# Decode attention with a gated MLP: one-hot products in place of small DMAs, and wq loaded in uneven strips

## The chip, the core and the metric

The kernel runs on one core of a Trainium2 chip. The metric is the device time of one execution in microseconds. A core has a matrix engine (PE, with weight loads listed as PEld), a vector engine (DVE), an activation engine (ACT), a general engine (POOL) and a queue engine (SP) which issues most of the DMAs. The DMAs run on 16 DMA engines. Matrix results land in PSUM; everything else is in SBUF, both with 128 partitions.

## The reference, cut to what matters

Two tokens (B = 2, one each) attend to a cache of 8 heads x 32,768 positions x 128, and the result is multiplied by a gate from a small MLP.

```python
x = A_x                                   # [2, 1, 512]
xn = _layernorm(x)
# attention: 32 query heads, 8 key/value heads, softmax over 32768 positions
q = (xn @ wq)                             # wq [512, 4096]
scores = einsum("bhqd,bhkd->bhqk", q, k) * Dh ** -0.5
o = einsum("bhqk,bhkd->bhqd", softmax(scores), v)
s = o.reshape(B, 1, Hq * Dh) @ wo         # wo [4096, 512]
# gate: an MLP on xn; with one position per token its token-mixing
# branch only sees the padding, so x1 = xn
h2 = _gelu(_layernorm(xn) @ w3) @ w4
g = _silu(xn + h2)
return x + s * g                          # [2, 1, 512]
```

## The kernel before

There are 16 groups, one for each pair of a token b and a key/value head k. The keys of a group are 32,768 x 128 bf16, 8 MB, and are laid out so that each partition holds 256 positions in a row of 65,536 bytes; the same goes for the values. The tile kbuf has three slots of 4 MB, vbuf two. One DMA of 128 rows loads the keys of a group (L398), one the values (L387); the last group is loaded in halves (L404, L392).

A loop on PE, DVE and ACT runs over the groups. DVE transposes blocks of the keys (L493), PE multiplies them with the query (L562), DVE finds the maxima (L476), ACT takes the exponential (L417), DVE turns the weights (L511), and PE multiplies them with the values (L584). PE's loop is one body that it branches back to; DVE's is a loop over pairs of groups; ACT, POOL and SP have their instructions written out for all groups.

The order of the loads is that of SP's queue. It first issues wq (L252) into the third slot of kbuf, w3 and w4 into vbuf (L253, L254) and the first keys (L255). Then, in turn, the values of a group, when PE has ended the products of the values before (L387, semaphore s_pv), and the keys of the next, when PE is half way through the scores (L398, semaphore s_half). Last come seven parts of wo (L411), the smaller ones at the end, and half of the store of the output (L523).

Before the loop comes a prologue. ACT's queue loads x (L258). DVE normalises it, PE turns it (L326) and multiplies it with wq, which waits for the semaphore of its load (L336); then come w3 (L357), a gelu, w4 (L372), and the gate g, two rows of 512 (L377). The output is computed in another layout: four partition quadrants, where partition 32n + b holds the columns 128n to 128n + 127 of token b. So x and g are needed there too. ACT's queue issues four DMAs of two rows for x into the tile x4_bf, which POOL has set to zero (L259, L270), and four of two rows for g into g4 (L267, L379). DVE casts x4_bf to f32 (L380).

The constants of the prologue are made by DVE from the identity matrix `ident` (L298 to L320).

After the loop PE computes the last head (L532) and multiplies the attention output with wo. The first KC = 2 of the eight row blocks of wo are multiplied in matmuls 512 wide into the PSUM tile qrb (L608); ACT copies that to SBUF as wsum (L519), and a product with `comb` brings it into the quadrants of `pro` (L623). The other blocks go straight into the quadrants, in matmuls 128 wide (L615). Each part waits for its own DMA. Then DVE multiplies with g4 and adds x4 (L520, L521), and SP and ACT store one token each (L523). The class LateQueue keeps PE's prologue instructions and places them ahead of the loop; a plain Queue records waits and counts.

Of the kernel before, what the change touches and what calls it, by code (L numbers as in the profile page):

```python
# [7 lines left out]
F32 = mybir.dt.float32  # L8
BF16 = mybir.dt.bfloat16
I32 = mybir.dt.int32  # L10
ACT = mybir.ActivationFunctionType
ALU = mybir.AluOpType
# [82 lines left out]
def kernel(  # L95
# [16 lines left out]
    B, Sq, D = A_x.shape  # L112
    _, Hkv, Sk, Dh = A_k_cache.shape
    HD = A_wq.shape[1]
# [4 lines left out]
    DK = D // 128  # L119
# [10 lines left out]
    NQ = 4  # L130
    QW = D // NQ
    QP = 32 * (NQ - 1) + B
# [6 lines left out]
    def sb(name, shape, dt):  # L139
        return pool.tile(shape, dt, name=name)  # L140
# [19 lines left out]
    xm = sb("xm", [128, NQ, rep], F32)  # L160
    z = sb("z", [128, NB, 2, ZC], BF16)
    x_bf = sb("x_bf", [B, D], BF16)
    x4_bf = sb("x4_bf", [128, QW], BF16)
    x4 = sb("x4", [128, QW], F32)
    g4 = sb("g4", [128, QW], F32)
    sg = sb("sg", [128, QW], F32)
    out4 = sb("out4", [128, QW], BF16)
    ident = sb("ident", [128, 128], BF16)
# [3 lines left out]
    cls = sb("cls", [128, NB, 2], F32)  # L172
    sel_o = sb("sel_o", [128, VT, rep], F32)
    quad = sb("quad", [128, 4], BF16)
    sel_h = sb("sel_h", [128, rep], F32)
    same_h = sb("same_h", [128, 128], F32)
    row_of = sb("row_of", [128, 32], F32)
# [20 lines left out]
    g = sb("g", [B, D], F32)  # L198
# [3 lines left out]
    sc = [bank(f"sc{i}") for i in range(NPART)]  # L202
# [4 lines left out]
    pro = bank("pro")  # L207
# [2 lines left out]
    groups = [(b, k) for b in range(B) for k in range(Hkv)]  # L210
    NG = len(groups)
    wo_parts = [(0, 4, 0, NQ), (4, 5, 0, NQ), (5, 6, 0, NQ), (6, 7, 0, NQ), (7, 8, 0, 2), (7, 8, 2, 3), (7, 8, 3, NQ)]
    KC = 2
    PAD = 24

    def sem(name):
        return tc.alloc_semaphore(name)

    def row_view(cache, b, k):
        return cache[b, k, :, :].rearrange("(p t) d -> p (t d)", p=128)  # L220

    sp = Queue(nc.sync, sem("s_sp"))
    ve = Queue(nc.vector, sem("s_ve"))
    ac = Queue(nc.scalar, sem("s_ac"))
    po = Queue(nc.gpsimd, sem("s_po"))
    pe = LateQueue(nc.tensor, sem("s_pe"))
    d_x, d_x4, d_wq, d_w3, d_w4, d_g, d_out = (
        sem(f"d_{n}") for n in ("x", "x4", "wq", "w3", "w4", "g", "out")
    )
    d_wo = [sem(f"d_wo{i}") for i in range(len(wo_parts))]  # L230
    t_T, t_z, t_mx, t_pt, t_ob, t_on = (sem(f"t_{n}") for n in ("T", "z", "mx", "pt", "ob", "on"))
    t_used, t_top, t_e, t_S, t_oT, t_xp = (sem(f"t_{n}") for n in ("used", "top", "e", "S", "oT", "xp"))
# [5 lines left out]
    kbuf_wq = kbuf[:, 2 * SLOT:3 * SLOT]  # L238
# [10 lines left out]

    with tc.tile_critical(sync_engine=mybir.EngineType.Pool, no_gpsimd_drain=True):  # L250

        sp.op(lambda e: e.dma_start(out=kbuf_wq[:, 0:DK * HD], in_=A_wq.rearrange("(p k) f -> p (k f)", k=DK)), inc=(d_wq, 16))  # L252
        sp.op(lambda e: e.dma_start(out=vbuf[:, 0:W4O], in_=B_w3.rearrange("(p k) f -> p (k f)", k=DK)), inc=(d_w3, 16))  # L253
        sp.op(lambda e: e.dma_start(out=vbuf[:, W4O:W4O + FK * D], in_=B_w4.rearrange("(p f) d -> p (f d)", f=FK)), inc=(d_w4, 16))  # L254
        sp.op(lambda e: e.dma_start(out=kbuf[:, 0:NPART * SLOT], in_=row_view(A_k_cache, *groups[0])), inc=(t_k[0], 16))  # L255
        nc.sync.sem_inc(t_k[1], 16)

        ac.op(lambda e: e.dma_start(out=x_bf[:, :], in_=A_x[:, 0, :]), inc=(d_x, 16))  # L258
        e_x4z = po.op(lambda e: e.memset(x4_bf[:, :], 0.0))  # L259
        e_xs0 = po.op(lambda e: e.memset(xs_bf[:, :], 0.0))  # L260
        e_id0 = po.op(lambda e: e.memset(ident[:, :], 0.0))
        e_id = po.op(lambda e: e.affine_select(
            out=ident[:, :], in_=ident[:, :], compare_op=ALU.not_equal, fill=1.0, base=0,
            pattern=[[-1, 128]], channel_multiplier=1), e_id0)
        e_ones = po.op(lambda e: e.memset(ones_f[:, :], 1.0))
        e_z0 = po.op(lambda e: e.memset(z[:, :, :, :], 0.0))
        e_g0 = po.op(lambda e: e.memset(g4[:, :], 0.0))  # L267
        po.op(lambda e: e.memset(ob[:, :], 0.0), inc=(t_ob, 1))
        for n in range(NQ):
            ac.op(lambda e, n=n: e.dma_start(out=x4_bf[32 * n:32 * n + B, :], in_=A_x[:, 0, n * QW:(n + 1) * QW]), e_x4z, inc=(d_x4, 16))  # L270


        ve.op(lambda e: e.memset(o[:, :], 0.0))
# [3 lines left out]
        e_s00 = ve.op(lambda e: e.memset(sc[1][:, :], 0.0))  # L277
        e = ve.op(lambda e: e.tensor_copy(out=xf[:, :], in_=x_bf[:, :]), (d_x, 16))
# [14 lines left out]
        e = e_xn = layernorm(xn, xf, "ln1", e)  # L293
        ve.op(lambda v: v.tensor_copy(out=xs_bf[0:B, :], in_=xn[:, :]), e_xn, e_xs0)
        e = layernorm(ln2, xn, "ln2", e_xn)
        e_xs = ve.op(lambda v: v.tensor_copy(out=xs_bf[32:32 + B, :], in_=ln2[:, :]), e)
        with nc.allow_low_precision(reason="one of the terms is one, the others are zero"):
            e = ve.op(lambda v: v.tensor_reduce(  # L298
                out=sel0[:, :], in_=ident[:, :].rearrange("p (n w e) -> p w n e", n=NB, e=2), axis=AX.XY, op=ALU.add), e_id)
# [6 lines left out]
            out=sel_o[:, :, :],  # L306
# [10 lines left out]
        ve.op(lambda v: v.tensor_scalar_mul(  # L317
            out=same_h[:, :].rearrange("p (r h) -> p r h", h=rep),
            in0=sel_h[:, :].unsqueeze(1).broadcast_to([128, 32, rep]), scalar1=-inv_sqrt_dh), e_selh)
        e_const = ve.op(lambda v: v.tensor_copy(  # L320
            out=sel_w[:, :, :], in_=row_of[:, :].unsqueeze(1).broadcast_to([128, 4, 32])), e_row)

# [9 lines left out]
        for i in range(NPART):  # L332
            for k in range(DK):
                for n in range(NQ):
                    last = k == DK - 1 and n == NQ - 1
                    e = pe.op(lambda t, i=i, k=k, n=n: t.matmul(  # L336
                        sc[i][32 * n:32 * n + B, :], lhsT=xT[:, k, :],
                        rhs=wq3[:, k, :].rearrange("p (h n y) -> p h n y", n=NQ, y=32)[:, i * HH:(i + 1) * HH, n, :],
                        start=(k == 0), stop=(k == DK - 1), tile_position=(0, 32 * n)),
                        e_xT, e_s00, (d_wq, 16), inc=last)  # L340
            e = ve.op(lambda v, i=i: v.transpose(out=qT[:, i * 512:(i + 1) * 512], in_=sc[i][:, :]), e)
        e_q = ve.op(lambda v: v.tensor_mul(
            out=q_sb[:, :, :, :].rearrange("p n e (b h) -> p (n e) b h", b=B),
# [31 lines left out]
        e_tf = ve.op(lambda v: v.tensor_add(out=t_f[:, :], in0=xn[:, :], in1=h2[0:B, :]), e_h2)  # L375
        e = ac.op(lambda v: v.activation(out=sig[:, :], in_=t_f[:, :], func=ACT.Sigmoid), e_tf)
        e_g = ve.op(lambda v: v.tensor_mul(out=g[:, :], in0=t_f[:, :], in1=sig[:, :]), e)  # L377
        for n in range(NQ):
            ac.op(lambda v, n=n: v.dma_start(out=g4[32 * n:32 * n + B, :], in_=g[:, n * QW:(n + 1) * QW]), e_g, e_g0, inc=(d_g, 16))  # L379
        e_x4 = ve.op(lambda v: v.tensor_copy(out=x4[:, :], in_=x4_bf[:, :]), (d_x4, 16 * NQ))  # L380
        ve.op(lambda v: v.memset(qrb[:, :], 0.0), e_qr)
        e_s0 = ve.op(lambda v: v.memset(pro[:, :], 0.0))

# [131 lines left out]
        e_oX[NG - 1] = head_out(last=True)  # L515


        e_ws, e_s = (pe.sem, pe.n + 1), (pe.sem, pe.n + 2)
        e_wsum = ac.op(lambda v: v.copy(out=wsum, in_=qrb[:, :]), e_ws)  # L519
        e = ve.op(lambda v: v.tensor_tensor(out=sg[0:QP, :], in0=pro[0:QP, 0:QW], in1=g4[0:QP, :], op=ALU.mult), (d_g, 16 * NQ), e_s)  # L520
        e = ve.op(lambda v: v.tensor_tensor(out=out4[0:QP, :], in0=sg[0:QP, :], in1=x4[0:QP, :], op=ALU.add), e, e_x4)  # L521
        for b, q in ((0, sp), (1, ac)):
            q.op(lambda v, b=b: v.dma_start(out=out[b, 0, :].rearrange("(n c) -> n c", c=QW), in_=out4[b:QP:32, :]), e, inc=(d_out, 16))  # L523
        sp.wait((d_out, 32))
# [2 lines left out]
        def head_oT(marks=None):  # L527
            take(nc.tensor, t_ob)
            for t in range(VT):
                if t == VT - 1 and marks:  # L530
                    marks.append(nc.tensor.mark_branch_hint_location())
                ins = nc.tensor.matmul(  # L532
                    oT[:, :], lhsT=ob[:, t * Dh:(t + 1) * Dh], rhs=sel_o[:, t, :],
                    start=(t == 0), stop=(t == VT - 1))
            ins.then_inc(t_oT, 1)
# [62 lines left out]
        with nc.body("pe_output", valid_engines=[PE]):  # L598

            marks = [nc.tensor.mark_branch_hint_location()]  # L600
            head_oT(marks)
            for i, (a, c, r0, r1) in enumerate(wo_parts):
                for k in range(a, c):
                    pe.wait(e_oX[(B - 1) * Hkv + k], (d_wo[i], 16))
                    for r in range(r0, r1):
                        gr = k * NQ + r
                        if k < KC:
                            pe.op(lambda t, k=k, r=r: t.matmul(  # L608
                                qrb[32 * r:32 * r + B, :], lhsT=oX[:, k, r, :], rhs=wo3[:, k, r * D:(r + 1) * D],
                                start=(k == 0), stop=(k == KC - 1), tile_position=(0, 32 * r)),  # L610
                                inc=(k == KC - 1 and r == NQ - 1))
                            continue
                        for n in range(NQ):
                            col = r * D + n * QW
                            pe.op(lambda t, k=k, r=r, n=n, col=col, gr=gr: t.matmul(  # L615
                                pro[32 * n:32 * n + B, 0:QW], lhsT=oX[:, k, r, :], rhs=wo3[:, k, col:col + QW],
                                start=(gr == KC * NQ), stop=(gr == Hkv * NQ - 1), tile_position=(0, 32 * n)),
                                inc=(gr == Hkv * NQ - 1 and n == NQ - 1))
                if i == 0:
                    take(nc.tensor, t_on)  # L620
                    head_xp()
                    for n in range(NQ):
                        pe.op(lambda t, n=n: t.matmul(  # L623
                            pro[32 * n:32 * n + B, 0:QW], lhsT=comb[:, :], rhs=wsum[:, n * QW:(n + 1) * QW],
                            start=False, stop=False, tile_position=(0, 32 * n)), e_wsum, inc=False)

            for _ in range(PAD):
                nc.tensor.wait_ge(d_wo[-1], 16)
            for n, mark in enumerate(marks):
                nc.tensor.br_ne(turn, 0, f"pe_output_{n}", "pe_groups").branch_hint(mark)  # L630
                nc.switch_bb(f"pe_output_{n}")
            nc.br("pe_done", engines=[PE])
# [31 lines left out]
```

## Time and profile before

| quantity | value |
|---|---|
| time, median of 3 runs | 657.79 us (657.18 to 658.07) |
| the profiled execution: its time, its span | 657.31 us, 655.5 us |
| granted PE clock, mean over the span | 0.81 |
| bytes read from HBM | 280.50 MB, 428 GB/s over the span |
| share of the 16 DMA engines' time on SP's queue (q1) | 99.0% |
| busy: PE, DVE, ACT, POOL | 409.6, 380.2, 39.5, 10.1 us |
| wq issued, first matmul that reads it | 0.89 us, 13.27 us |
| first values issued (L387) | 29.20 us |
| g sent to the quadrants (L379), four issues | 31.35 us, 2.50 us in all |
| wo issued: first part, seven issues | 616.81 us, over 22.97 us |
| multiply with g4, add of x4, store issued (start) | 651.55, 651.88, 652.19 us |

The span runs from the first to the last instruction of the profiled execution; what lies around it, 1.8 us, belongs to the time but is not in the profile. Times in the profile's lines are in microseconds, a mean in nanoseconds. In a line of the timeline the start comes first, then the duration, the engine, the line of the kernel, the operation, the tiles out<-in, the shape and the count; in brackets is the idle time of the engine before it and what ended it. "SPq" and "ACTq" are the queues that issue DMAs: their durations are the time of the issue, not of the transfer. In a table of stretches each row has the stretch, its length, the busy time of PE, PEld, DVE, ACT and POOL with counts, the granted clock, the busy share of the 16 DMA engines and the rate in GB/s.

The opening of the timeline, cut to the queues' issues and to the first matmul that reads wq:

```profile
0.89 0.39 SPq L252 DMA_DIRECT2D kbuf<-in_A_wq_dram  x1
0.90 0.55 ACTq L258 DMA_DIRECT2D x_bf<-in_A_x_dram  x1
1.34 0.41 SPq L253 DMA_DIRECT2D vbuf<-in_B_w_dram  x1
1.50 1.24 ACTq L270 DMA_DIRECT2D x_bf<-in_A_x_dram  x4
1.80 0.51 SPq L254 DMA_DIRECT2D vbuf<-in_B_w_dram  x1
2.35 0.52 SPq L255 DMA_DIRECT2D kbuf<-in_A_k_cache_dram  x1
13.27 3.58 PE L336 MATMUL sc<-kbuf,xT 128*2 128x512 bf16 x32 [4.07 <-DMA kbuf<-in_A_wq_dram]
29.20 0.33 SPq L387 DMA_DIRECT2D vbuf<-in_A_v_cache_dram  x1
31.35 2.50 ACTq L379 DMA_DIRECT2D g<-g  x4
```

### The profile page before, as it was taken

What the parts mean: (1) busy time and instruction counts of PE and PEld (TensorE: products, weight loads), DVE (VectorE), ACT (ScalarE), POOL (GpSimd) and SP (SyncE); (2) the same over time, 40 slices, a digit from 0 to 9 for tenths busy, and PEclk for the clock granted to TensorE, in tenths of its full rate; (3) what the DMA queues carried; (4) which work ended last, traced back from release to release, by engine and by line L of the source; (5) the groups of instructions that cost most, each with busy time, mean ns of one, the idle gap of its engine ahead of it and who ended that gap; (6) DMA issues with size and microseconds to landing.
All of it is one profiled execution on the core that took longest, in us unless ns stands there. A gap on an engine that the chain in (4) does not pass through costs nothing. (4 is left out here: it accounts for less than half of the span.)

```text
span 655.5 us, 6482 instructions
## 1 busy us (share of the span) xinstructions
PE 409.6 (62%) x2444; PEld 164.1 (25%) x2444; DVE 380.2 (58%) x534; ACT 39.5 (6%) x89; POOL 10.1 (2%) x43
## 2 busy tenths in 40 slices
PE   2528386564938656494765749566383856648765
PEld 0113132231313212131321313232131322213323
DVE  5348194673819457291855729285482937638770
ACT  1100101000010000001000000100001010000100
POOL 1000000000000000000000000000000000000000
PEclk9859677696987769697686969878696887979798
DMA  8999999999999999999999999999999999999996
GB/s 365 435 449 444 445 420 420 444 444 444 396 448 444 444 428 412 448 440 444 416 428 444 440 448 400 444 444 440 440 404 448 440 444 420 424 444 414 448 418 262
DMA packets 6779, 280.58 MB, mean 428 GB/s; under 512 B 746, under 2 KB 1012, under 8 KB 2036
## 3 DMA queue, kind: packets, MB, share of 16 engines
q1 hardware_dynamic: 6728, 280.50, 99.0%
q8 instruction: 2, 0.03, 0.0%
q14 instruction: 5, 0.04, 0.0%
q10 hardware_dynamic: 44, 0.01, 0.0%
HBM read 280.50 MB, written 0.00 MB: 428 GB/s over the span
## 5 line engine op out<-in xcount | busy, mean ns | idle before, releaser
L493 DVE STREAM_TRANSPOSE T<-kbuf 128x1024 int32<-128x1024 int32 x256 | 295.7, 1214 | 186.7 <-DVEq L473 186.4
L562 PE MATMUL sc<-T,z 128*128 128x512 bf16 x1024 | 280.2, 422 | 164.9 <-PEq L473 161.8
L562 PEld LDWEIGHTS sc<-T,z 128*128 128x128 bf16 x1024 | 98.8, 104 | 330.1 <-issue 251.7
L584 PE MATMUL o<-vbuf,pt 128*16 128x512 bf16 x1024 | 90.8, 533 | 35.0 <-PEq L473 35.0
L584 PEld LDWEIGHTS o<-vbuf,pt 128*16 128x16 bf16 x1024 | 34.3, 117 | 85.8 <-issue 78.4
L417 ACT ACTIVATE ep<-sc,shift 128x512 bf16<-128x512 f32 x32 | 21.7, 682 | 479.8 <-DVE shift L503 479.8
L511 DVE STREAM_TRANSPOSE pt<-ep 128x512 bf16<-128x512 bf16 x32 | 22.6, 708 | 15.3 <-DVEq L473 15.3
L476 DVE TENSOR_REDUCE mx<-sc 128x1 f32<-128x512 f32 x32 | 21.5, 672 | 15.7 <-DVEq L473 15.7
L574 PE MATMUL S<-mxr,same_h 128*128 128x64 f32 x32 | 6.5, 284 | 22.0 <-PEq L473 22.0
L532 PEld LDWEIGHTS oT<-sel_o,ob 128*128 128x128 f32 x136 | 17.7, 191 | 3.2 <-issue 0.5
L532 PE MATMUL oT<-sel_o,ob 128*128 128x4 f32 x136 | 16.2, 243 | 0.5 <-PEq L473 0.5
L420 ACT COPY ob<-o 128x512 f32<-128x512 f32 x16 | 9.4, 585 | 97.0 <-PE o L584 97.0
L574 PEld LDWEIGHTS S<-mxr,same_h 128*128 128x128 f32 x32 | 4.8, 188 | 29.8 <-issue 29.8
L438 POOL COPY oX<-oXs 128x4 bf16<-128x4 bf16 x15 | 2.8, 188 | 520.8 <-DVE oXs L470 520.8
L478 DVE TENSOR_SCALAR mxr<-row_of,mx 128x32 f32<-128x32 f32 x32 | 7.7, 241 | 4.8 <-DVEq L473 0.3
L503 DVE TENSOR_REDUCE shift<-S 128x1 f32<-128x64 f32 x16 | 3.6, 225 | 11.2 <-DVEq L473 11.2
L591 PEld LDWEIGHTS S<-sm,ones_f 128*128 128x128 f32 x32 | 4.8, 188 | 6.9 <-issue 6.9
L372 PE MATMUL sc<-vbuf,h_bf 128*2 128x512 bf16 x14 | 4.8, 521 | 2.4 <-DVE h_bf L369 2.4
L417 ACT ACTIVATION_READ_ACCUMULATOR ep<-sc,shift 128x1 f32 x32 | 6.3, 196 | 0.0
L427 POOL TENSOR_TENSOR z<-qr,quad 128x64 bf16<-128x64 bf16 x16 | 4.7, 292 | 102.2 <-DVE shift L503 86.4
L591 PE MATMUL S<-sm,ones_f 128*128 128x8 f32 x32 | 6.2, 266 | 0.0
L336 PE MATMUL sc<-kbuf,xT 128*2 128x512 bf16 x32 | 3.6, 627 | 4.1 <-DMA kbuf<-in_A_wq_dram 4.1
(88 smaller groups left out, 63.6 us busy)
## 6 DMA issues: line engine op xcount, KB each, us to landing
kbuf<-in_A_k_cache_dram SPq DMA_DIRECT2D x2, 4096.0 KB, 21.7
vbuf<-in_A_v_cache_dram SPq DMA_DIRECT2D x2, 4096.0 KB, 20.2
kbuf<-in_A_wq_dram SPq DMA_DIRECT2D x1, 4096.0 KB, 12.3
vbuf<-in_B_w_dram SPq DMA_DIRECT2D x2, 1792.0 KB, 18.0
kbuf<-in_A_wo_dram SPq DMA_DIRECT2D x1, 2048.0 KB, 29.3
kbuf<-in_A_wo_dram SPq DMA_DIRECT2D x3, 512.0 KB, 30.8
kbuf<-in_A_wo_dram SPq DMA_DIRECT2D x1, 256.0 KB, 31.7
kbuf<-in_A_wo_dram SPq DMA_DIRECT2D x2, 128.0 KB, 15.6
```

Of the source, the lines that this page charges most:

```text
L372: e_h2 = pe.op(lambda t, f=f: t.matmul(h2[0:B, :], lhsT=h_bf[:, f * B:(f + 1) * B], rhs=w4v[:, f, :], start=(f == 0), stop=(f == FK - 1)), ...
L417: ac.op(lambda v, i=i: v.activation(out=ep[i][:, :], in_=sc[i][:, :], func=ACT.Exp, scale=inv_sqrt_dh, bias=shift[:, :], accum_out=rs[:, i ...
L420: ac.op(lambda v: v.copy(out=ob[:, :], in_=o[:, :]), (s_pv, m + 1), inc=(t_ob, 1))
L476: nc.vector.tensor_reduce(out=mx[:, i:i + 1], in_=sc[i][:, :], axis=AX.X, op=ALU.max).then_inc(t_d, 1)
L478: ins = nc.vector.tensor_scalar_mul(out=mxr[:, i, :], in0=row_of[:, :], scalar1=mx[:, i:i + 1])
L493: nc.vector.transpose(out=Ts[n % T_BUFS][:, :].rearrange("p (b t k) -> p t b k", b=NB, t=RT), in_=kt[:, r * W:(r + 1) * W].rearrange("p (t ...
L511: nc.vector.transpose(out=pt[h][:, :, :].rearrange("p r (t h) -> p t r h", h=rep), in_=ep[order(par).index(h)][:, :].rearrange("p (t r h) ...
L532: ins = nc.tensor.matmul(oT[:, :], lhsT=ob[:, t * Dh:(t + 1) * Dh], rhs=sel_o[:, t, :], start=(t == 0), stop=(t == VT - 1))
L562: ins = nc.tensor.matmul(sc[i][:, :], lhsT=z[:, nb, w, zc:zc + 128], rhs=Tb[:, nb, :, w], start=(r == 0 and nb == 0 and w == 0), stop=(r = ...
L574: nc.tensor.matmul(S[:, NPART * rep:], lhsT=same_h[:, :], rhs=mxr[:, :, :].rearrange("p i r -> p (i r)"), start=True, stop=True).then_inc( ...
L584: ins = nc.tensor.matmul(o[32 * j:32 * j + VT * rep, :], lhsT=pt[h][:, r, a * VT * rep:(a + 1) * VT * rep], rhs=vt[:, u * VT:(u + 1) * VT, ...
L591: nc.tensor.matmul(S[:, 0:NPART * rep], lhsT=ones_f[:, :], rhs=sm[:, :, :].rearrange("p i h -> p (i h)"), start=True, stop=True).then_inc( ...
```

## The change

The eight small DMAs that bring x and g into the quadrants go, with the tile x4_bf, the two memsets on POOL and the cast on DVE. In their place PE multiplies, after the last head's products and ahead of wo, the rows of x with a piece of the identity (two ones, bf16), and the rows of g with the same in f32 (`one_f`, copied by DVE among the constants). Eight matmuls write x and g for the four quadrants into the PSUM bank sc[0]; ACT copies them into x4 and g4 ahead of wsum. The final multiply waits for these copies.

KC is 3 instead of 2: one more row block of wo goes through qrb and wsum.

The load of wq becomes 13 DMAs. One brings the first 8,192 of the 16,384 columns (16 KB of each partition's row) on 128 partitions. The rest comes in four strips of 2,048 columns (4 KB a row), each as a DMA of partitions 0 to 111 and two of the last 16 partitions, split 8 and 8, 12 and 4, 14 and 2, 10 and 6. The matmuls at L336 wait for all of them.

```diff
-    x4_bf = sb("x4_bf", [128, QW], BF16)
+    one_f = sb("one_f", [B, 32], F32)
...
-    KC = 2
+    KC = 3
+    CP = 2048
+    C0 = DK * HD - 4 * CP
+    wq_parts = [(0, 128, 0, C0)]
+    for i, r in enumerate((8, 12, 14, 10)):
+        wq_parts += [(a, b, C0 + i * CP, C0 + (i + 1) * CP) for a, b in ((0, 112), (112, 112 + r), (112 + r, 128))]
...
-        sp.op(lambda e: e.dma_start(out=kbuf_wq[:, 0:DK * HD], in_=A_wq.rearrange("(p k) f -> p (k f)", k=DK)), inc=(d_wq, 16))
+        for r0, r1, c0, c1 in wq_parts:
+            sp.op(lambda e, r0=r0, r1=r1, c0=c0, c1=c1: e.dma_start(
+                out=kbuf_wq[r0:r1, c0:c1], in_=A_wq.rearrange("(p k) f -> p (k f)", k=DK)[r0:r1, c0:c1]), inc=(d_wq, 16))
...
-        e_x4z = po.op(lambda e: e.memset(x4_bf[:, :], 0.0))
...
-        e_g0 = po.op(lambda e: e.memset(g4[:, :], 0.0))
...
-        for n in range(NQ):
-            ac.op(lambda e, n=n: e.dma_start(out=x4_bf[32 * n:32 * n + B, :], in_=A_x[:, 0, n * QW:(n + 1) * QW]), e_x4z, inc=(d_x4, 16))
...
+        ve.op(lambda v: v.tensor_copy(out=one_f[:, :], in_=ident[0:B, 0:32]))
...
-                        e_xT, e_s00, (d_wq, 16), inc=last)
+                        e_xT, e_s00, (d_wq, 16 * len(wq_parts)), inc=last)
...
-        for n in range(NQ):
-            ac.op(lambda v, n=n: v.dma_start(out=g4[32 * n:32 * n + B, :], in_=g[:, n * QW:(n + 1) * QW]), e_g, e_g0, inc=(d_g, 16))
-        e_x4 = ve.op(lambda v: v.tensor_copy(out=x4[:, :], in_=x4_bf[:, :]), (d_x4, 16 * NQ))
...
-        e_ws, e_s = (pe.sem, pe.n + 1), (pe.sem, pe.n + 2)
+        e_xg, e_ws, e_s = ((pe.sem, pe.n + i) for i in (1, 2, 3))
+        for t, dst in enumerate((x4, g4)):
+            e_x4 = ac.op(lambda v, t=t, dst=dst: v.copy(out=dst[:, :], in_=sc[0][:, t * QW:(t + 1) * QW]), e_xg)
...
-        e = ve.op(lambda v: v.tensor_tensor(out=sg[0:QP, :], in0=pro[0:QP, 0:QW], in1=g4[0:QP, :], op=ALU.mult), (d_g, 16 * NQ), e_s)
-        e = ve.op(lambda v: v.tensor_tensor(out=out4[0:QP, :], in0=sg[0:QP, :], in1=x4[0:QP, :], op=ALU.add), e, e_x4)
+        e = ve.op(lambda v: v.tensor_tensor(out=sg[0:QP, :], in0=pro[0:QP, 0:QW], in1=g4[0:QP, :], op=ALU.mult), e_x4, e_s)
+        e = ve.op(lambda v: v.tensor_tensor(out=out4[0:QP, :], in0=sg[0:QP, :], in1=x4[0:QP, :], op=ALU.add), e)
...
+            for t, (lhs, rhs) in enumerate(((ident[0:B, 0:32], x_bf), (one_f[:, :], g))):
+                for n in range(NQ):
+                    pe.op(lambda v, t=t, lhs=lhs, rhs=rhs, n=n: v.matmul(
+                        sc[0][32 * n:32 * (n + 1), t * QW:(t + 1) * QW], lhsT=lhs, rhs=rhs[:, n * QW:(n + 1) * QW],
+                        start=True, stop=True, tile_position=(0, 32 * n)), e_g, inc=t == 1 and n == NQ - 1)
```

More of the change, by code (lines that the diff above doesn't have):

```diff
@@ L226 @@
     pe = LateQueue(nc.tensor, sem("s_pe"))
-    d_x, d_x4, d_wq, d_w3, d_w4, d_g, d_out = (
-        sem(f"d_{n}") for n in ("x", "x4", "wq", "w3", "w4", "g", "out")
-    )
+    d_x, d_wq, d_w3, d_w4, d_out = (sem(f"d_{n}") for n in ("x", "wq", "w3", "w4", "out"))
     d_wo = [sem(f"d_wo{i}") for i in range(len(wo_parts))]
```

## The prediction

> **What bounds the kernel now.** First the page's engine shares and slices.
>
> ```profile
> span 655.5 us, 6482 instructions
> PE 409.6 (62%) x2444; PEld 164.1 (25%) x2444; DVE 380.2 (58%) x534; ACT 39.5 (6%) x89; POOL 10.1 (2%) x43
> DMA  8999999999999999999999999999999999999996
> DMA packets 6779, 280.58 MB, mean 428 GB/s; under 512 B 746, under 2 KB 1012, under 8 KB 2036
> ```
>
> No engine passes 62%, while the DMA engines are full in 38 of 40 slices. Next, the waits of the SP queue (time in total, times, longest) and the DMA issues with the median time to landing:
>
> ```profile
> SPq L387 <- PE o L584: 281.7, 14, 20.7
> SPq L398 <- PE sc L562: 229.9, 13, 19.0
> ...
> kbuf<-in_A_k_cache_dram SPq DMA_DIRECT2D x15, 27.2
> vbuf<-in_A_v_cache_dram SPq DMA_DIRECT2D x15, 26.4
> ```
>
> SP waits for PE before each load, but a load then needs 27 us to land while 8 MB takes 8 x 2.414 = 19.3 us per lane (below): some 8 us of earlier work is still queued at each issue, so the DMA engines never starve. The trace's packet records (queue, start, duration, bytes) show it finely. On one DMA engine the next packet starts 3 to 4 ns before the last one ends, so the records string into 16 lanes. In each, packets follow without a gap from 1.9 us to the end, and one costs about 5 ns + 0.0368 ns per byte: 65,536 B 2.414 us, 32,768 B 1.209, 4,096 B 0.155, a semaphore write 0.006. The end of the kernel is the end of the last lane. Busy time by stretch there (DMA share and GB/s are last):
>
> ```profile
> 649.00:649.25 0.25, 0.19 (x16) 0.00 (x0) 0.00 (x0) 0.00 (x0) 0.00 (x0) 1.00 1.06 377
> 649.25:649.50 0.25, 0.00 (x0) 0.00 (x0) 0.00 (x0) 0.00 (x0) 0.00 (x0) 1.00 0.86 307
> 649.50:649.75 0.25, 0.00 (x0) 0.00 (x0) 0.00 (x0) 0.00 (x0) 0.00 (x0) 1.00 0.69 225
> 649.75:650.00 0.25, 0.02 (x4) 0.05 (x6) 0.00 (x0) 0.00 (x0) 0.00 (x0) 1.00 0.23 82
> 650.00:650.25 0.25, 0.25 (x16) 0.19 (x16) 0.00 (x0) 0.00 (x0) 0.00 (x0) 1.00 0.20 70
> 650.50:651.00 0.50, 0.34 (x12) 0.19 (x12) 0.00 (x0) 0.00 (x0) 0.00 (x0) 1.00 0.09 35
> ```
>
> A share of 0.20 is three lanes of 16. Lane A ends at 650.91, B at 650.54, C at 650.31, the 13 others between 649.31 and 649.85; the mean is 649.72. The three are late because instruction fetches ran on them: 16,384 B at 71.9 us on A (0.96 us, and the packet after it took 2.886 instead of 2.418), 8,192 B at 35.8 us on B (0.31, then 2.955), 8,192 B at 265.3 us on C (0.31, then 2.662). C is also one of the two lanes (call them the pair) that carried every two-row DMA of L270 and L379. A's last packet frees the last matmuls, then VectorE and the store:
>
> ```profile
> 650.94 0.09 PEld L615 LDWEIGHTS pro<-kbuf,oX 128*2 128x2 bf16 x4 [0.21 <-DMA kbuf<-in_A_wo_dram]
> 651.55 0.29 DVE L520 TENSOR_TENSOR sg<-pro,g 98x128 f32<-98x128 f32 x1 [3.12 <-PE pro L615]
> 651.88 0.29 DVE L521 TENSOR_TENSOR out<-sg,x 98x128 bf16<-98x128 f32 x1
> 652.19 0.64 SPq L523 DMA_DIRECT2D out_dram<-out  x1
> ```
>
> From 650.91 to the span's end is 4.6 us. So the change is worth what it does to the last of 16 lane ends, and to this tail.
>
> **The strips of wq.** Half of wq goes in one DMA of 128 rows of 16 KB, eight rows per lane. The other half goes in four strips of 4 KB rows: each strip 112 rows (seven per lane), then r and 16-r rows with r = 8, 12, 14, 10, at most one row per lane. If a DMA of r rows takes the first r lanes of a fixed order, as the two-row DMAs always took the pair, the lanes get c = 8, 8, 7, 7, 6, 6, 5, 5, 3, 3, 2, 2, 1, 1, 0, 0 extra rows; an even split is 4. A lane's wq now costs 8 x 1.209 + 0.006 = 9.678 us. After: 8 x 0.607 (worked out from the 5 ns + bytes line) + (28 + c) x 0.1555 + (5 + c) x 0.006. The difference is -0.44 us at c = 0, +0.21 at the mean c = 4 (smaller packets), +0.69 at 7, +0.86 at 8. Every lane then carries its difference to the end, as it carries the fetches now.
>
> [...]
>
> **The DMAs of x and g that go.** Four of L270 and four of L379 put one row and one semaphore write each on both lanes of the pair: a 256 B row held the lane up by 14 ns, a 512 B row by 23, a write by 6. That is 4 x 20 + 4 x 29 = 0.20 us off the pair, nothing off A or B. The 2.5 us of issuing at L379 leave the ACT queue, which is next needed for the first group's Exp at 66.4 us (L417): no gain.
>
> **Sum of the lanes.** C, of the pair: 650.31 + 0.86 - 0.20 = 650.97. A is not of the pair: 650.91 plus -0.44 to +0.69, unknown where. B: 650.10 to 651.23. Others: at most 649.85 + 0.69 = 650.54. With A at c = 0 to 3 (four of seven values) C takes over and the end moves by +0.06; with c = 5, 6, 7 by +0.37, +0.53, +0.69. I take +0.06 and keep -0.44 (if C's fetch falls elsewhere) and +0.69 for the range.
>
> **Issue time on SP.** Twelve more DMAs at 0.39 to 0.64 us (L252 to L255 and L523) put the w3 issue at 0.89 + 13 x 0.45 = 6.7 us, or 9.2 at the dear end; 1.04 us from issue to first packet (0.89 to 1.93) makes 10.3. The lane with least work has wq until 1.9 + 0.7 (cold first packet) + 9.2 = 11.8. So w3, w4 and K0 queue in time; SP is next wanted at 29.20 (L387). Gone cover would cost up to 0.5 us. wq lands about 0.7 us later on the pair, so PE starts L336 at 14 instead of 13.27 and V0 is issued at 30 instead of 29.2; K0 occupies the lanes until 40.2.
>
> **Tail.** On PE, eight source matmuls go before L608: four bf16 like L615 (16 in 0.39: 0.10 us) and four f32 like L623 (eight in 0.40), 0.5 to 0.6 together. KC = 3 adds four 512-wide matmuls (eight took 0.60: +0.30) and removes sixteen 128-wide (-0.39).
>
> ```profile
> 646.24 0.60 PE L608 MATMUL qrb<-kbuf,oX 128*2 128x512 bf16 x8 [0.65 <-DMA kbuf<-in_A_wo_dram]
> 646.90 0.59 ACT L519 COPY T<-qrb 128x512 f32<-128x512 f32 x1 [2.47 <-PE qrb L608]
> 647.54 0.40 PE L623 MATMUL pro<-T,comb 128*2 128x128 f32 x8
> 648.79 0.39 PE L615 MATMUL pro<-kbuf,oX 128*2 128x128 bf16 x16 [0.63 <-DMA kbuf<-in_A_wo_dram]
> 649.98 0.39 PE L615 MATMUL pro<-kbuf,oX 128*2 128x128 bf16 x16 [0.80 <-DMA kbuf<-in_A_wo_dram]
> ```
>
> The one-hot products fit the 0.65 us that PE idles before L608. ACT copies two 128x128 tiles, each between 0.2 (a small ACTIVATE) and 0.59 (L519), while L608 runs; wsum then starts at about 647.2, L623 behind it at 647.9 instead of 647.5. PE idles 0.63, 0.80 and 0.25 us before later parts, so 1.7 us of slip is covered; without cover the tail would lengthen by at most 0.6 + 0.4 = 1.0. DVE (cast for cast) and POOL (two memsets fewer) are off the path.
>
> **Do the strips run at line rate?** Every load of before covers 128 partitions; seven rows per lane is shown nowhere. Lower bound: 0.155 us a row, as in the wo packets, +0. Upper bound from the slowest packets: the first sixteen of wq took 1.91 us on average instead of 1.213, a factor 1.57; on 32 x 0.155 = 4.98 us that is +2.8. Evidence for the lower end: the eight 512 B rows of g went, from the pair, into partitions that other lanes also write, and no K packet from 36.2 to 56.9 us took anything but 2.418. But 512 B might hide in a buffer. I take +0.
>
> [...]
>
> **Sum.** The profiled execution took 657.31 us (span 655.5, 1.8 around it): 657.31 + 0.06 = 657.37. The median of the three runs is 657.79, 0.48 above it: forecast 657.9, own range 657.3 to 658.5.
>
> **Rivals.**
> Lanes evened: C's fetch falls on another lane, or the extra rows do, and A and B are low in c. [...] The end falls by 0.44 and at best to the mean, 649.72 + 0.21, -1.0: 656.8 to 657.4.
> [...]
> Late tail: part 0 of wo no longer finds PE idle and the slip is not made good: up to +1.0, 658.9. Against: 1.7 us of idle PE behind.
> The change doesn't do what it says: the r rows spread evenly, c = 4 everywhere; then A ends +0.21 later, 658.0, inside the forecast's range.
>
> **How the numbers follow.** Forecast with its range (the even spread included) 0.47; slow strips 0.35; lanes evened 0.14; late tail 0.04. 0.2% is 1.3 us, about what a measurement of this kernel can tell from no change. Slower: slow strips and a part of the late tail, 0.38. Faster: evening cannot reach 656.5 by its own floor, but what the fetches do from run to run is unknown, 0.09. Same: 0.53. Range 656.9 to 661.0.
>
> **What would show it.** Lane ends: C near 650.97 as last or beside A; 4,096 B packets of wq at 159 ns (right) or 200 and more (slow strips); wq landing at 13.5; DMA share falling over 1.5 us at the end as before (right) or in under 0.8 (evened); idle PE before the later parts of wo. Packets of wq above 0.2 us would make the prediction wrong.

## The result, and the profile after

The changed kernel takes 660.90 us (median of 6 runs, 660.64 to 661.08) against 657.51 us of the kernel before in the same comparison: a ratio of 1.0051, with a 95% interval from 1.0038 to 1.0064. It is slower by 3.4 us. The profiled execution took 661.08 us, with a span of 658.8 against 655.5. One execution of a kernel further down (the same destination, another source) took 698.02 us, in a slow state, and is left out of its median.

The page after, engine shares and DMA:

```profile
span 658.8 us, 6485 instructions
PE 410.0 (62%) x2444; PEld 164.0 (25%) x2444; DVE 380.1 (58%) x534; ACT 39.9 (6%) x91; POOL 9.8 (1%) x41
DMA  9999999999999999999999999999999999999996
DMA packets 7386, 280.57 MB, mean 426 GB/s; under 512 B 850, under 2 KB 1108, under 8 KB 2644
```

Nearly the same bytes, and DMA engines as busy as before, in a longer span. Busy is not the same as moving. Busy time by stretch at the start shows it; the last two columns are the busy share of the DMA engines and GB/s. First, two stretches of the kernel before, while its one DMA of wq runs:

```profile
4.00:6.00 2.00, 0.00 (x0) 0.00 (x0) 1.52 (x6) 0.25 (x2) 0.00 (x0) 1.00 1.02 442
...
10.00:12.00 2.00, 0.00 (x0) 0.00 (x0) 0.73 (x6) 0.00 (x0) 0.00 (x0) 1.00 1.03 443
```

Then the changed kernel:

```profile
4.00:6.00 2.00, 0.00 (x0) 0.00 (x0) 1.52 (x6) 0.20 (x1) 0.00 (x0) 1.00 1.02 434
...
8.00:10.00 2.00, 0.29 (x4) 0.21 (x4) 1.93 (x11) 0.70 (x1) 0.00 (x0) 1.00 1.05 289
10.00:12.00 2.00, 0.00 (x0) 0.00 (x0) 0.64 (x6) 0.00 (x0) 0.00 (x0) 1.00 1.05 272
12.00:14.00 2.00, 0.00 (x0) 0.00 (x0) 0.00 (x0) 0.00 (x0) 0.00 (x0) 1.00 1.03 277
```

From 4 to 6 us the first half of wq comes in at 434 GB/s. While the strips run, all 16 lanes are busy, but at 272 to 289 GB/s: each packet takes longer. The trace's packet records (start, duration, bytes of each packet) give the size: the 512 packets of 4,096 B of the strips took 234 ns on the mean, where 159 is the undisturbed duration (893 of the 896 packets of that size in wo took it before). That is 75 ns x 32 packets = 2.40 us per lane. And the loss goes on into the next load: the packets of w3 and w4, all 535 ns before, cost 0.71 us more per lane, almost all of it in the first two of each lane. This outlasts the strips themselves: the last strip packet ended at 15.89 us, and a w3 packet that began at 15.93 still took 859 ns. The 16 lanes end at 652.85 us on the mean, 3.12 later than before, and the last one at 653.95, 3.04 later.

The timeline at the start and at the end (most lines are left out):

```profile
0.89 4.99 SPq L256 DMA_DIRECT2D kbuf<-in_A_wq_dram  x13
5.92 0.36 SPq L258 DMA_DIRECT2D vbuf<-in_B_w_dram  x1
16.93 3.58 PE L338 MATMUL sc<-kbuf,xT 128*2 128x512 bf16 x32 [7.89 <-DMA kbuf<-in_A_wq_dram]
...
648.57 0.23 PE L605 MATMUL sc<-x_bf,ident 2*32 2x128 bf16 x4
648.64 0.39 PE L605 MATMUL sc<-g,one_f 2*32 2x128 f32 x8
649.10 0.27 ACT L519 COPY x<-sc 128x128 f32<-128x128 f32 x1 [1.63 <-PE sc L605]
649.34 0.82 PE L614 MATMUL qrb<-kbuf,oX 128*2 128x512 bf16 x12 [0.31 <-DMA kbuf<-in_A_wo_dram]
650.84 0.40 PE L629 MATMUL pro<-T,comb 128*2 128x128 f32 x8 [0.35 <-ACT T L520]
653.06 0.39 PE L621 MATMUL pro<-kbuf,oX 128*2 128x128 bf16 x16 [0.84 <-DMA kbuf<-in_A_wo_dram]
654.60 0.23 PE L621 MATMUL pro<-kbuf,oX 128*2 128x128 bf16 x4 [0.36 <-DMA kbuf<-in_A_wo_dram]
```

The first matmul that reads wq starts at 16.93 us instead of 13.27. At the end the one-hot products lie ahead of the first part of wo, and PE still waits for a DMA before the later parts: the end is the end of the DMA stream, as before.

### The profile page after: what moved, and what is told of

Read it like the earlier page. It is cut to its first block, busy times and chain, and to the rows that moved or that the text cites. A ratio compares the mean times of both kernels' runs of the same rounds, so it can differ in the third digit from the quotient of the medians.

```text
span 658.8 us, 6485 instructions
## 1 busy us (share of the span) xinstructions
PE 410.0 (62%) x2444; PEld 164.0 (25%) x2444; DVE 380.1 (58%) x534; ACT 39.9 (6%) x91; POOL 9.8 (1%) x41
## 5 line engine op out<-in xcount | busy, mean ns | idle before, releaser
L343 DVE STREAM_TRANSPOSE T<-sc 128x512 f32<-128x512 f32 x2 | 1.4, 717 | 9.2 <-PE sc L338 9.2
```

## The experiments

Each one starts from the changed kernel and alters only how wq arrives, except where said. The ratio is to the kernel before, in the same comparison. The diffs show the lines that matter; "..." marks what is left out.

**One DMA for wq.** Is it the strips, or the rest of the change?

```diff
...
-    wq_parts = [(0, 128, 0, C0)]
-    for i, r in enumerate((8, 12, 14, 10)):
-        wq_parts += [(a, b, C0 + i * CP, C0 + (i + 1) * CP) for a, b in ((0, 112), (112, 112 + r), (112 + r, 128))]
+    wq_parts = [(0, 128, 0, DK * HD)]
```

> wq in one DMA of 128 rows again, the one-hot products and KC = 3 stay. If the strips alone made the kernel slower: the last DMA lane ends as before (lane A, about 650.9 us; C about 0.2 us earlier), time within 0.4 us of before, 657.1 to 657.9. If the one-hot products or the longer tail took a part: 658.5 or more, with the time from the last lane's end to the span's end above 5 us.

Measured 657.78 us, ratio 1.0000 (0.9990 to 1.0009); the last lane ends at 651.07. The one-hot products, KC = 3 and the eight DMAs that went make together no difference that can be seen within this interval, 0.6 us either way: the loss is in the strips.

**Four even strips of 128 rows.**

```diff
-        wq_parts += [(a, b, C0 + i * CP, C0 + (i + 1) * CP) for a, b in ((0, 112), (112, 112 + r), (112 + r, 128))]
+        wq_parts += [(0, 128, C0 + i * CP, C0 + (i + 1) * CP)]
```

> The same half of wq in four strips of 4 KB rows, but each strip as one DMA of 128 rows, eight per lane. Theory of the destination (lanes that take seven-row shares write into partitions that share a path): 4,096 B packets of wq back at 159 ns, wq lands near 13.0 us, time 0.2 us above before, 657.5 to 658.0. Theory of the source (4 KB pieces, one every 32 KB of HBM, are read slowly): packets at 234 ns as in the changed kernel, wq lands near 15.5 us, time about 660. Theory of the many small DMAs: 657.5 to 658.0 as well.

Measured 657.90 us, ratio 1.0004 (0.9995 to 1.0014). All 512 packets took 159 ns. The timeline and the stretches:

```profile
13.24 3.58 PE L338 MATMUL sc<-kbuf,xT 128*2 128x512 bf16 x32 [4.21 <-DMA kbuf<-in_A_wq_dram]
```

```profile
8.00:10.00 2.00, 0.29 (x4) 0.21 (x4) 1.93 (x11) 0.69 (x1) 0.00 (x0) 1.00 1.01 414
10.00:12.00 2.00, 0.00 (x0) 0.00 (x0) 0.64 (x6) 0.00 (x0) 0.00 (x0) 1.00 1.04 426
```

So neither the size of 4 KB nor its pitch of 32 KB in HBM is slow here: the packets of wo, 4,096 B too, took the same 159 ns.

**112 rows and 16 rows.** Every lane gets seven rows and one: even, and no DMA on few lanes.

```diff
...
+        wq_parts += [(a, b, C0 + i * CP, C0 + (i + 1) * CP) for a, b in ((0, 112), (112, 128))]
```

> Each strip as 112 rows and 16 rows: seven and one row per lane, so every lane has the same load and no DMA uses few lanes. Destination: packets still above 200 ns on the mean, wq lands at 15 to 16 us, time 659.8 to 660.9. Unevenness or few-lane DMAs as the cause: packets at 159 ns, time 657.5 to 658.1. Source: 234 ns, about 660.

Measured 660.93 us, ratio 1.0046 (1.0029 to 1.0063), packets of 247 ns on the mean: as slow as the changed kernel, without any unevenness.

```profile
10.00:12.00 2.00, 0.00 (x0) 0.00 (x0) 0.64 (x6) 0.00 (x0) 0.00 (x0) 1.00 1.03 254
```

What costs is the split of a strip into 112 rows and the rest. How uneven the rest is makes no difference in the time that can be seen (660.93 against 660.90).

**64 rows and 64 rows.** Half of the partitions at a time.

```diff
...
+        wq_parts += [(a, b, C0 + i * CP, C0 + (i + 1) * CP) for a, b in ((0, 64), (64, 128))]
```

> Each strip as partitions 0 to 63 and 64 to 127: four rows per lane in each, even. [...] Source: 234 ns, about 660. Few-lane DMAs or unevenness: 159 ns, 657.5 to 658.0.

Measured 661.45 us, ratio 1.0055 (1.0038 to 1.0072). The packets took 261 ns on the mean, 273 after the first 128 of 512, and the stretches show a little over half of the 443 GB/s of the kernel before:

```profile
10.00:12.00 2.00, 0.00 (x0) 0.00 (x0) 0.64 (x6) 0.00 (x0) 0.00 (x0) 1.00 1.03 240
12.00:14.00 2.00, 0.00 (x0) 0.00 (x0) 0.00 (x0) 0.00 (x0) 0.00 (x0) 1.00 1.06 250
```

The theory of the destination gave the direction, but the author's estimate from it, 311 ns (twice the 155.5 ns that a 4,096 B packet holds its lane) and 662.6 us, was too much for the mean; that two lanes share a path, which it assumes, no run shows. The 273 ns hide a pattern. After the first 128 the packets took 211 to 315 ns, 102 of 384 took 300 or more, and in each lane the durations repeat almost exactly every four packets, which is the number of rows that a lane has in one of these DMAs (when consecutive packets are chained into lanes, the correlation at a distance of four is 0.98). The slowest, up to 315 ns, took about twice the undisturbed 159. What sets the four durations is open; no run isolates it.

**The same destination, another source.** Each 64-row DMA reads 64 neighbouring pieces of 4 KB in HBM. The strips then hold other parts of wq (i counts the pieces of 256 KB), so the query computed from them is another one, at the same cost.

```diff
...
+    for i in range(4):
+        wq_parts += [(a, b, C0 + i * CP, C0 + (i + 1) * CP) for a, b in ((0, 64), (64, 128))]
...
+        def wq_src(r0, r1, c0, c1):
+            if r1 - r0 == 128:
+                return A_wq.rearrange("(p k) f -> p (k f)", k=DK)[r0:r1, c0:c1]
+            i = 2 * ((c0 - C0) // CP) + r0 // 64
+            return A_wq.rearrange("d (s c) -> (d s) c", c=CP)[64 * i:64 * i + 64, :]
...
-                out=kbuf_wq[r0:r1, c0:c1], in_=A_wq.rearrange("(p k) f -> p (k f)", k=DK)[r0:r1, c0:c1]), inc=(d_wq, 16))
+                out=kbuf_wq[r0:r1, c0:c1], in_=wq_src(r0, r1, c0, c1)), inc=(d_wq, 16))
```

> The strips of 64 and 64 partitions again, with the destination unchanged and another source: each DMA reads 64 pieces of 4 KB that lie one after the other in HBM instead of 32 KB apart (so that these columns of wq hold other data of wq). Destination: packets at 273 ns as with the 64-row strips before, time 661.0 to 661.9. Source rows as the cause: 159 ns, 657.5 to 658.3.

Measured 661.50 us, ratio 1.0062 (1.0041 to 1.0082), packets of 264 ns on the mean, again 273 after the first ones, in the same pattern of four.

```profile
10.00:12.00 2.00, 0.00 (x0) 0.00 (x0) 0.64 (x6) 0.00 (x0) 0.00 (x0) 1.00 1.06 248
```

The source rows are not the cause. What is left is the destination: which partitions the lanes write at a time. The next pair tests that directly.

**14 rows, 9 partitions apart, and 14 neighbours.** Only the last 2,048 columns of wq come in strips here: nine DMAs of 14 rows and one of 2. The two kernels have the same number of DMAs, rows and bytes, and differ only in which partitions a DMA takes. (The rows of wq in HBM go with the partitions; the experiment before found that they do not matter there, 264 ns against 261.)

```diff
...
+    wq_parts += [(slice(j, j + 118, 9), C0, DK * HD) for j in range(9)] + [(slice(126, 128), C0, DK * HD)]
```

> Seven eighths of wq in one DMA of 128 rows, the last 2,048 columns in nine DMAs of 14 rows and one of 2, the 14 rows 9 partitions apart. Uneven (lanes get 9 or 10 rows, two lanes none), many few-lane DMAs, 4 KB rows; but no two lanes of a DMA write near partitions. Destination: packets of 4,096 B at 159 ns, two lanes 1.2 us early, the others about 0.25 us late, time 0.1 to 0.4 us above the kernel with one DMA, 657.7 to 658.3. Few-lane DMAs or unevenness as the cause: packets above 200 ns, 658.5 or more.

```diff
...
+    wq_parts += [(slice(14 * j, 14 * j + 14), C0, DK * HD) for j in range(9)] + [(slice(126, 128), C0, DK * HD)]
```

> The same ten DMAs with the same number of rows, bytes and lanes, but each takes 14 neighbouring partitions. [...] Any theory that leaves the partitions out: the same as with 9 partitions between the rows.

9 apart: 658.63 us, ratio 1.0017 (1.0008 to 1.0027), packets with a median of 159 ns and a mean of 186. Neighbours: 659.56 us, ratio 1.0029 (1.0019 to 1.0040), median 243, mean 236. The intervals overlap a little, the runs do not (highest 659.05, lowest 659.27). The order is as the theory of the destination has it, and both sizes were missed; for the neighbours the author's estimate was 546 ns, twice the 273 of the 64 rows, and 660 to 661.5 us, with a number of lanes on one path that no run shows. So the partitions make 0.9 us of difference between two kernels that are otherwise alike. Neighbours cost less than that; a lane writes only 36 KB here, and the first 64 of the 128 packets still averaged 191 ns. And 9 apart is not free: 658.63 lies in the range that its expectation gave to few-lane DMAs or unevenness as the cause, though the packets, half of them at 159 ns, do not bear that out. The packet records say when the loss comes: up to 11.95 us all strip packets but one (191) took 159 ns. Two lanes have no strip rows and go on to w3 at 11.81, and from then on the strip packets of the others grow to 442 ns and the first w3 packets to 1,215. So the loss comes while some lanes carry the strip and others w3; why, no run isolates, and unevenness stays a rival for this part.

**Twelve rows, 9 partitions apart, in 1 KB pieces.** A try at an uneven split that pays.

```diff
...
+    CP = 512
...
+    wq_parts += [(slice(j, j + 100, 9), C0, DK * HD) for j in range(9)]
+    wq_parts += [(slice(108, 124), C0, DK * HD), (slice(124, 128), C0, DK * HD)]
```

> Can an uneven split without shared paths beat one DMA? In the trace of the changed kernel the latest lane (the 16 KB instruction fetch) is one of those that got one extra row, so the 13th or 14th in order. Here the last 512 columns go in nine DMAs of 12 rows, 9 partitions apart, and two small ones: the last four lanes carry one row of 1 KB instead of eight. Latest lane 0.29 us earlier, the next one 0.2 us later: the end moves by about -0.15 us, time 657.3 to 657.9, not to be told from one DMA. If the lane was placed wrongly: +0.15 to +0.2, 657.7 to 658.2.

Measured 658.60 us, ratio 1.0015 (1.0005 to 1.0024): a miss, above both ranges of its expectation and slower than the kernel before. The strip packets took 46 ns as they should, and the last lane ended at 651.24, but all lanes were later: 650.46 on the mean against 649.60 with one DMA. The w3 packets carry 0.61 us of that; twelve lanes show packets of 1.06 to 1.40 us instead of 0.535 between 13.6 and 14.1 us. What holds them up there stays open.

## Why the prediction went as it did

Its likeliest case was wrong, its largest rival happened. The forecast of 657.9 us had the strips at line rate; slow strips, the rival with a chance of 0.35, stood at 660.6, the prediction's upper bound of +2.8 us on the median of 657.79. The time lies inside the stated range, up to 661.0, only because that rival had been let in, and by 0.1 us: that is no merit of the forecast's mechanism. By the prediction's own sign, "Packets of wq above 0.2 us would make the prediction wrong", the 234 ns decide against it.

- **The step that failed** is "Do the strips run at line rate?", where the price was bounded by 0 and 2.8 us and "I take +0". Measured are 2.40 us in the strip packets and 0.71 in the w3 and w4 packets behind them, 3.1 together: above the upper bound, because the packets of the next load are slow too, which no bound had.
- **The evidence that misled it** was the eight rows of g, 512 B each, that slowed nobody (every K packet from 36.2 to 56.9 us took 2.418). The changed kernel's own packets show why that was no test: the first 64 packets of the strips, about four per lane or 16 KB, also took 159 ns (159.5 on the mean), and only the later ones 212 to 293 (means of 64). So 512 B say nothing about 128 KB per lane. Why the first ones pass is open; no run shows it. The prediction doubted the 512 B itself and still priced the doubt at nothing.
- **What the partitions do** is known here by durations alone: 128 rows 159 ns, 64 rows 273 on the mean after the first packets, 14 neighbours 236 against 186 for 14 rows 9 apart, and 264 against 261 with another source for the 64 rows. How lanes come to slow one another, by a shared path or otherwise, no run shows, neither for the rival of slow strips nor for the theory of the destination; the runs show in its place that the strips' packets took 234 ns instead of 159.
- **Which lanes get the extra rows** was right as far as the packets show: chained into lanes, the 16 carried between 28 and 36 strip packets, and wq ended on them from 14.25 us (28) to 15.89 (36). Lane A, with the 16,384 B fetch (now at 77.1 us), had one extra row, B seven, C eight. Any evening by the extra rows is lost in the strips' own cost.
- **SP's issues** were cheaper than reckoned, 4.99 us for 13, and w3 was issued at 5.92, not 6.7. No lane starved (the busy share of the 16 from 4 to 20 us is 1.01). PE reads wq at 16.93 instead of the forecast 14: the slow strips again. It costs nothing, since the keys arrive later: the first land at 45.38 us, and PE idles 15.59 us before the scores at 48.04.
- **The tail** went as forecast: the one-hot products ran from 648.57 to 649.03, in the gap before the first part of wo; ACT's copies took 0.27 us each; later parts still found PE waiting (0.84 and 0.36 us). The last lane's end is 4.9 us from the span's end, against 4.6 before and 4.6 with one DMA for wq. With the 3.04 us of the last lane these 0.26 us make up the whole 3.30 by which the span grew. The landing records place them: the last landing of wo comes 0.60 us after the last lane's end (653.95 to 654.55), against 0.31 before (650.91 to 651.23) and with one DMA (651.07 to 651.39). On that lane an instruction fetch of 8,192 B and 309 ns begins right behind the last semaphore write. In the twelve-row kernel the lane with that fetch behind it ended at 651.21, and the last landing came at 651.78, 0.57 later. Whether the fetch holds the landing up is not shown; no run moves it away.
- **The DMAs taken away** were forecast to take 0.20 us off the pair of lanes and nothing off the end by themselves. The kernel with one DMA for wq shows no gain that can be seen.

## What to carry to other kernels

When DMA lanes are the bound, a busy share of 100% can hide packets that take half as long again (here 234 ns against 159, at a share of 1.03 to 1.05): compare the duration of one packet with that of an undisturbed packet of the same size, and look at how the durations spread before you reason from their mean. A load in DMAs over fewer than the 128 partitions cost far more here than the imbalance it was to mend (3 us against at most 1.2, the 650.91 of the last lane less the mean of 649.72), and the load queued behind it paid as well (0.71 us a lane). Cut loads along the free dimension, with all 128 rows in each DMA (four such strips kept 159 ns and 657.90 us), and move work between lanes only after measuring such a split by itself.

## What was not expected of the hardware

- The loss shows late and lasts. In the changed kernel about four packets (16 KB) per lane pass at 159 ns first, with 64 and 64 rows only two or three, and afterwards the next DMA's packets are slow too (up to 1.12 us instead of 0.535 in the changed kernel).
- With 64 and 64 rows the packets of a lane repeat a pattern of four durations between 211 and 315 ns. The mean of 273 hides this.
- What a DMA costs to issue differed with its rows. The eleven issues of wq took SP 8.23 us with rows 9 partitions apart and 4.77 with neighbouring rows, 0.75 against 0.43 us each. Spacing is not all of it: the nine issues of the kernel with 64 neighbouring rows took 5.64 us, 0.63 each.
- In the changed and the twelve-row kernel an instruction fetch started right behind a lane's last semaphore write, and the last landing came 0.60 and 0.57 us after that lane's end, against 0.31 before and with one DMA.
